# A third of w_out's K as seven block products, with sums by adding DMAs and seeded banks

## The chip, the cores and the metric

The kernel runs on one core of a Trainium2 chip. The metric is the device time of one execution in microseconds (us), as the median of three runs. One profiled execution of the same kernel gives the trace from which all rows below are read.

## The reference, cut to what matters

```
attn = windowed attention of q, k, v (4 batches, 8 heads, 576 positions, 64 wide; window 64)
x  = attn as 2304 rows of 512
g  = x @ w_gate                      # 512 -> 1536
h  = silu(g) * (x @ w_val)
x2 = h @ w_out                       # 1536 -> 512
a, b = x2 @ w1, x2 @ w2              # 512 -> 1024 each
out = ((a * b) @ w3) @ w_out2        # 1024 -> 1024 -> 512
```

The activations are float32, the weights arrive as float64. The kernel holds each value as two float32r words, a high one and a rest, and multiplies in three passes: high by high, high by rest, rest by high.

## The kernel before, in words

**Stages.** The 2304 tokens are three *token pairs* (tp 0 to 2) of two blocks of T = 384 tokens. Attention comes first, then gated layer 1 (`gated` with silu), `project` (h times w_out), gated layer 2 (a times b), the product of w3 and w_out2 (accumulators `acc`, L992), and the final product (L1067, L1135). TensorE goes through them one after another, and DVE, ACT and the DMA queues prepare operands for it: narrow the float64 words of a weight (L194, L197, L203, L207), cast to the high word (L218), subtract to get the rest (L227), and load and store.

**Gated layers.** A unit is one pair of blocks of columns of one weight for one token pair; layer 1 has 36 units, layer 2 has 24. A unit is already computed as seven block products instead of eight (Strassen-Winograd's sums), each of two 128-deep parts by three passes, six matmuls of 128x128 by 128x384. The accumulators are PSUM banks: `al` takes products 1, 6, 7, 4 in turn, `be` takes 5 and 3, `ga` takes 2. `al` after product 1 is copied out by ACT with its sign changed (tile c11, or the h tile `ha` itself for the gate), and DVE adds `ga` to it (L681). The products of neighbouring units are interleaved by the table `AT`, so that between two products of one unit others stand. `plan.wait(self.read)` makes the program reach a modelled time, nothing more; on the chip each matmul that overwrites or adds to a bank waits for the reader of that bank.

**project.** For each token pair 12 pieces of K (f) by 4 blocks of columns (m) by 2 token blocks (x) by 3 passes: 288 matmuls at L834, all eight PSUM banks accumulating over the whole K. The rows of h come back from DRAM: `Rows.queue` loads 384 KB pieces (pl, L793, on SP's queue), ACT casts them (ph<-pl, 128x768), DVE subtracts the rest in place. There are 36 such pieces. w_out is narrowed and split while layer 1 runs, stored to DRAM (`by_wo`), and loaded again as 16 resident tiles `wo` (L1288).

**Order.** The order is written by a planner, `Plan`: it keeps a model clock for each engine, and emits jobs (with costs, ranks, due times and SBUF slots) to DVE, ACT, SP and a queue called DMA (POOL's, used for DMAs that add into SBUF, L236) as TensorE's model time advances; `plan.need` forces a job that TensorE needs now. SP's DMAs go round a ring of eight: each waits for the one issued eight earlier. Each engine's instructions then stand in this order.

Of the kernel before, what the change touches and what calls it, by code (L numbers as in the profile page):

```python
# [17 lines left out]
P = 128  # L18
# [15 lines left out]
AT = {1: 0, 2: 2, 5: 3, 6: 4, 7: 8, 4: 12, 3: 13}  # L34
# [3 lines left out]
def window_attention_moe_kernel(ctx: ExitStack, tc: tile.TileContext, q, k, v, w_gate, w_val, w_out, w1, w2, w3, w_out2, out):  # L38
# [13 lines left out]
    NSLOT = 56  # L52
# [5 lines left out]
    half = ctx.enter_context(tc.tile_pool(name="half", bufs=7))  # L58
# [27 lines left out]
    class Job:  # L86
        def __init__(self, fn, after=(), cost=None, lag=0.0, rank=0, slots=0, due=0.0, early=False):

            self.rank, self.slots, self.due, self.early = rank, slots, due, early
            self.fn, self.after, self.cost, self.lag, self.done = fn, [x for x in after if x], cost, lag, None  # L90

    class Plan:
        def __init__(self):
            self.now, self.since, self.ahead, self.queue = 0.0, 0.0, 0.0, []
            self.free = dict.fromkeys(engines, 0.0)
            self.shut = set()
            self.rank, self.landing, self.early = 0, 6.0, False

            self.slots, self.keep = NSLOT - ATTENTION, 0

        def job(self, fn, after=(), lag=LAG, slots=0, due=0.0, early=False, **cost):
            j = Job(fn, after, cost, lag, self.rank, slots, due, early)
# [14 lines left out]
        def emit(self, j, e):  # L117
            start = max([self.free[e], self.since] + [x.done for x in j.after])
            self.queue.remove(j)
            j.fn(engines[e])  # L120
# [8 lines left out]
        def fill(self, but):  # L129
            limit = self.now + self.ahead  # L130
            while True:
                best = None
                for e, free in self.free.items():
# [3 lines left out]
                    for j in self.queue:  # L137
                        if e not in j.cost or (j.early and e == "DVE" and not self.early) or any(x.done is None for x in j.after):
                            continue
                        if j.slots and self.slots < j.slots + self.keep:  # L140
# [35 lines left out]
    def pool(n):  # L176
        return 0.1 + 0.0026 * n
# [7 lines left out]
    def narrow(part, load, due):  # L185
# [7 lines left out]
        n = 512  # L193
# [17 lines left out]
    def cast(hi, src, after, n, slots=1, negate=False, due=0.0):  # L211
        def fn(eng):
# [4 lines left out]
            else:  # L217
                (eng.copy if eng is nc.scalar else eng.tensor_copy)(out=hi(), in_=src())  # L218
        return plan.job(fn, after, slots=slots, due=due, early=True, ACT=act(n), DVE=0.1 + 0.0006 * n,
                        **({} if negate else {"POOL": pool(n)}))  # L220

    def rest(lo, src, hi, after, n, slots=0, negate=False, due=0.0):
        if negate:
# [4 lines left out]
                        after, slots=slots, due=due, DVE=dve(n), POOL=pool(n))  # L228

    def combine(out, x, y, op, after, n, due=0.0):  # L230
        return plan.job(lambda eng: eng.tensor_tensor(out=out(), in0=x(), in1=y(), op=op), after, due=due,  # L231
                        DVE=dve(n), POOL=pool(n))
# [5 lines left out]
    def loading(fn, after=(), slots=0, lag=9.0):  # L238
        return plan.job(fn, after, lag=lag, slots=slots, SP=0.5)
# [4 lines left out]
    class Doubles:  # L244
# [26 lines left out]
        def narrowed(self):  # L271
            return [narrow(lambda j=j: self.st[:, 512 * j:512 * j + 512], self.loaded[j], self.due) for j in range(2)]
# [4 lines left out]
    class Weights(Doubles):  # L277
# [19 lines left out]
        def make(self):  # L297
# [7 lines left out]
            for p in PRODUCTS:  # L305
                after, due = ready if p in sums else [ready[at[p][1] - 1]], self.due + AT[p]
                if p in sums:
                    x, y, op = sums[p]
                    after = [combine(lambda p=p: self.words(*at[p]), lambda x=x: self.words(*x),
                                     lambda y=y: self.words(*y), op, after + [made.get({6: 5, 3: 6}.get(p))], n, due)]  # L310
# [5 lines left out]
                         [a], n, not (p == 3 and self is left2[max(left2)]), p == 4, due)  # L316
# [9 lines left out]
    class Operands:  # L326
# [5 lines left out]
        def __init__(self, x, name, after=None, by_dma=(), rest_by_dma=(), due=0.0):  # L332
# [9 lines left out]
            for p in PRODUCTS:  # L342
                for m in range(2):
                    wait, when = [after[p]] if after else [], due + AT[p]
                    if p in sums:
# [4 lines left out]
                                combine(to, to, of, ALU.add, wait, T, when)]  # L350
# [11 lines left out]
                    else:  # L362
                        b = rest(lo, lambda m=m, p=p: blk(m, *at[p]), hi, [a], T, due=when)
# [271 lines left out]

    def gated(xop, left, order, func, hd, events, apart=0):
# [20 lines left out]
        class Unit:  # L657
# [26 lines left out]
            def put(self, i, t, src):  # L684

                h, direct = self.h(i, t), (i, t) == (1, 0)
                if self.x and direct:
# [8 lines left out]
                elif direct:  # L696
                    negated(h, src)
                    plan.charge("ACT", act(T))
# [8 lines left out]
            def product(self, p):  # L707
                if p == 1:
# [5 lines left out]
                    self.c11 = self.own(0, 0, "c11")  # L714
                    later(1, lambda: self.copy(self.c11, self.al))
                elif p == 2:
                    ga = bank(f"ga{self.name}")[:, :T]
                    self.mm(ga, 2, True)
                    self.add(self.c11, self.c11, ga)
# [732 lines left out]
```

## Time and profile before

| what | value |
|---|---|
| median of 3 runs | 825.04 us (824.42 to 825.47) |
| span of the profiled execution | 822.8 us |
| time around that span, by the median | about 2.2 us |
| TensorE (PE) busy | 811.8 us, 99% |
| VectorE (DVE) busy | 637.4 us, 77% |
| ScalarE (ACT) busy | 455.1 us, 55% |
| GpSimd (POOL) busy | 90.8 us, 11% |
| bytes moved by DMA | 140.23 MB |

The page of the profile gives the span from the first to the last instruction. The profiled execution has no time of its own beside the span; the difference to the median of the runs is taken as the launch and end, the same before and after.

### The profile page before, as it was taken

Reading aid. Unit: us, or ns where it says so; the run is one execution under the profiler, and the core shown is the slowest. Engines: PE = TensorE matmul, PEld = TensorE weight load, DVE = VectorE, ACT = ScalarE, POOL = GpSimd, SP = SyncE. Lnnn points to the kernel's source line nnn. Section 1 sums busy time; section 2 is a strip of 40 time slices with the busy share of each in tenths; the row PEclk is TensorE's granted clock in tenths of the full one; section 3 lists DMA queues with packets and bytes.
Section 4 is the critical chain, followed back from the end, with each engine's and each line's share of the span. In section 5 each row is a group of like instructions: output and inputs, shape, how many; then the busy total and the mean of one; then the engine's idle time right before and its main releaser. Section 6 shows DMA issues by size and latency. Waiting matters only on the chain.

```text
span 822.8 us, 15571 instructions
## 1 busy us (share of the span) xinstructions
PE 811.8 (99%) x5702; PEld 783.5 (95%) x5702; DVE 637.4 (77%) x1353; ACT 455.1 (55%) x1194; POOL 90.8 (11%) x135
## 2 busy tenths in 40 slices
PE   7999999999999999999999999999999999999998
PEld 5777899999999999999999999999999998899997
DVE  5899898686887959866888683877888844789994
ACT  6899997555556445633663551444444423655543
POOL 3666842000000000000000000000010110000000
PEclk9999999999999999999999999999999999999999
DMA  9999295253562444599987712024565289107632
GB/s 187 195 200 197 46 238 113 90 192 129 192 222 79 148 154 179 210 360 403 373 264 175 231 57 103 29 83 134 166 205 157 108 295 325 37 3 207 182 71 78
DMA packets 172765, 140.23 MB, mean 170 GB/s; under 512 B 120848, under 2 KB 142608, under 8 KB 171664
## 3 DMA queue, kind: packets, MB, share of 16 engines
q1 hardware_dynamic: 167888, 125.86, 50.6%
q0 software_dynamic: 4800, 13.37, 5.9%
q8 instruction: 45, 0.74, 0.4%
q14 instruction: 32, 0.26, 0.1%
HBM read 92.27 MB, written 42.99 MB: 164 GB/s over the span
## 4 chain that ended last, share of the span: by engine, by line
PE 91%; ACT 4%; SPq 2%; DMA 2%; DVE 1%; issue 0%; POOL 0%; ACTq 0%
PE o L834 18%; PE ala L669 15%; PE alb L669 15%; PE bea L669 8%; PE beb L669 8%; PE acc L992 5%; PE al L1135 4%; PE gaa L669 4%; PE gab L669 4%; ACT pexp L480 2%; PE be L1135 2%; PE al L1067 2%; PE PV L519 1%; SPq L403 1%; PE be L1067 1%; PE ga L1135 1%
## 5 line engine op out<-in xcount | busy, mean ns | idle before, releaser
L834 PE MATMUL o<-ph,wo 128*128 128x384 f32 x576 | 146.2, 334 | 0.0
L834 PEld LDWEIGHTS o<-ph,wo 128*128 128x128 f32 x576 | 103.9, 188 | 0.0
L834 PE MATMUL o<-pl,wo 128*128 128x384 f32 x288 | 96.2, 334 | 0.0
L377 ACT ACTIVATE ha<-ala 128x384 f32<-128x384 f32 x102 | 49.5, 489 | 50.1 <-PE ala L669 49.5
L759 POOL DMA_DIRECT2D h<-ha x24 | 13.0, 544 | 548.2 <-DVE ha L691 548.2
L681 DVE TENSOR_TENSOR ha<-ha,bea 128x384 f32<-128x384 f32 x60 | 33.1, 551 | 38.5 <-PE bea L669 22.1
L834 PEld LDWEIGHTS o<-pl,wo 128*128 128x128 f32 x288 | 54.1, 188 | 0.0
L480 ACT ACTIVATE pexp<-S,stat 128x128 f32<-128x128 f32 x144 | 53.3, 428 | 0.0
L218 ACT CAST hf<-h 128x384 fp32r<-128x384 f32 x84 | 38.7, 514 | 14.4 <-DVE h L231 13.6
L694 ACT ACTIVATE ha<-ha 128x384 f32<-128x384 f32 x54 | 28.3, 526 | 32.4 <-DVE ha L681 32.4
L227 DVE TENSOR_TENSOR hf<-h,hf 128x384 fp32r<-128x384 f32 x84 | 42.2, 545 | 4.9 <-ACT hf L218 4.8
L227 DVE TENSOR_TENSOR pl<-pl,ph 128x768 fp32r<-128x768 f32 x36 | 33.4, 953 | 13.2 <-ACT ph L218 12.8
L218 ACT CAST ph<-pl 128x768 fp32r<-128x768 f32 x36 | 29.2, 837 | 25.1 <-DMA pl<-h 22.6
L490 POOL TENSOR_TENSOR pexp<-pexp,stat 128x384 f32<-128x384 f32 x48 | 39.0, 833 | 36.4 <-DVE stat L487 18.0
L377 ACT ACTIVATE c12b<-alb 128x384 f32<-128x384 f32 x30 | 14.8, 493 | 50.3 <-PE alb L669 50.0
L480 ACT ACTIVATION_READ_ACCUMULATOR pexp<-S,stat 128x1 f32 x144 | 38.1, 267 | 0.0
L681 DVE TENSOR_TENSOR c22b<-c22b,beb 128x384 f32<-128x384 f32 x30 | 16.6, 553 | 25.8 <-ACT c22b L377 25.8
L669 PE MATMUL ala<-xo,w_g_7h 128*128 128x384 f32 x120 | 30.3, 336 | 0.5 <-ACT ha L377 0.5
L473 DVE TENSOR_REDUCE stat<-S 128x3 f32<-128x384 f32 x48 | 24.4, 550 | 7.6 <-PE S L466 7.4
L669 PE MATMUL ala<-xo,w_g_1h 128*128 128x384 f32 x126 | 29.2, 335 | 0.0
L218 ACT CAST xp<-X 128x384 fp32r<-128x384 f32 x42 | 19.7, 519 | 10.9 <-DVE X L231 8.0
L377 ACT ACTIVATE c11b<-alb 128x384 f32<-128x384 f32 x30 | 14.7, 489 | 19.5 <-PE alb L669 19.5
(625 smaller groups left out, 2453.2 us busy)
## 6 DMA issues: line engine op xcount, KB each, us to landing
h<-ha SPq DMA_DIRECT2D x36, 384.0 KB, 3.0
pl<-h SPq DMA_DIRECT2D x36, 384.0 KB, 6.3
h<-ha POOLq DMA_DIRECT2D x24, 384.0 KB, 3.2
h<-h SPq DMA_DIRECT2D x24, 384.0 KB, 6.4
st_w<-in_moe_w_dram SPq DMA_DIRECT2D x8, 1024.0 KB, 6.5
st_wo<-in_moe_w_out_dram SPq DMA_DIRECT2D x6, 1024.0 KB, 5.1
wo<-by_wo SPq DMA_DIRECT2D x12, 512.0 KB, 4.1
st_g<-in_moe_w_gate_dram SPq DMA_DIRECT2D x5, 1024.0 KB, 5.2
```

The source lines that it names most:

```text
L218: (eng.copy if eng is nc.scalar else eng.tensor_copy)(out=hi(), in_=src())
L227: return plan.job(lambda eng: eng.tensor_tensor(out=lo(), in0=src(), in1=hi().bitcast(F32), op=ALU.subtract), after, slots=slots, due=due, ...
L377: nc.scalar.mul(out=out, in_=in_, mul=-1.0)
L480: nc.scalar.activation(out=pe[:, jj, :], in_=so[:, jj, :], func=AF.Exp, bias=st[:, 0, x, jj:jj + 1], accum_out=st[:, 1, x, jj:jj + 1])
L490: nc.gpsimd.tensor_tensor(out=pe, in0=pe, in1=st[:, 3, x, :].unsqueeze(2).to_broadcast([P, SUB, P]), op=ALU.mult)
L669: nc.tensor.matmul(acc, lhsT=self.wt.ops[p, x][:, m, :], rhs=self.xs.ops[p, m][:, y, :], start=start and n == 0, stop=n == 5, skip_group_c ...
L681: nc.vector.tensor_tensor(out=out, in0=x, in1=y, op=ALU.add)
L694: nc.scalar.activation(out=h, in_=src, func=func, scale=-1.0 if direct else 1.0)
L834: nc.tensor.matmul(acc[m, x], lhsT=wos.tiles[i // 6][:, i % 6, :], rhs=rows[2 * tp + x].words(f, b), start=f == n == 0, stop=f == NF - 1 a ...
L992: nc.tensor.matmul(acc, lhsT=w3T[i][c // 3][:, x, (c % 3) * P:(c % 3) * P + P], rhs=zt[c, y], start=c == k == 0, stop=c == NI - 1 and k == 2)
L1067: nc.tensor.matmul(acc, lhsT=self.xs.ops[p, m][:, x, t * P:t * P + P], rhs=right.ops[p, m, y], start=start and n == 0, stop=n == 3 * R - 1 ...
L1135: nc.tensor.matmul(acc, lhsT=right.ops[p, m, y][:, P * k:P * k + P], rhs=self.xs.ops[p, m][:, x, :], start=bool(name) and n == 0, stop=n = ...
```

## The change

**w_out.** Of the six pairs of K (256 each) the first two (one pair of pairs, with fp 0 and 1) are multiplied as seven block products per token pair. Each product is two halves of its columns by two 128-deep parts of K by three passes, 12 matmuls; the third of K costs 7 x 12 = 84 matmuls per token pair where it cost 96 of 288. The other four pairs are multiplied plainly, block by block, 192 matmuls per token pair, and added into the same banks: `STEPS` is the order, numbers for products, pairs (i, j) for plain blocks. `ga` starts as ACT's copy of `al` after product 1, `de` as its copy after product 7. In all 276 matmuls per token pair instead of 288. The rows are now 15 pieces of 384 KB per token pair (7 products' sums and 8 plain ones), and w_out 20 tiles of 384 KB.

**The sums of h.** For fp 0 and 1, `spread` has ACT make one more copy of a block, and four DMAs that add in SBUF (on POOL's queue) make the sums, each followed by its store: 24 adding DMAs in all.

**Seeded banks in the gated layers.** From the seventh unit of each layer on, the copy of `al` after product 1 goes into the bank `ga`, and product 2 accumulates there; the DVE add of c11 falls away. `AT` now places product 5 ahead of product 2. Layer 2 needs an ACT copy for h in its place where x is 0.

**The rest.** Layer 2's operands get two sums and two rests from adding DMAs (24 more). Weights are narrowed 1024 words at a time. SBUF slots 58 instead of 56, `half` buffers 5 instead of 7. The cast and rest jobs lose POOL as a choice, which was closed to them before, too. TensorE has 36 matmuls fewer in all.

```
-AT = {1: 0, 2: 2, 5: 3, 6: 4, 7: 8, 4: 12, 3: 13}
+AT = {1: 0, 5: 2, 2: 3, 6: 4, 7: 8, 4: 12, 3: 13}
...
-    NSLOT = 56
+    NSLOT = 58
...
-    half = ctx.enter_context(tc.tile_pool(name="half", bufs=7))
+    half = ctx.enter_context(tc.tile_pool(name="half", bufs=5))
...
         def narrowed(self):
-            return [narrow(lambda j=j: self.st[:, 512 * j:512 * j + 512], self.loaded[j], self.due) for j in range(2)]
+            if self.second is None:
+                return [narrow(lambda: self.st, self.loaded[0], self.due, 1024)] * 2
...
+                    self.seeded = len(xs) > SEEDED
+                    self.ga = bank(f"ga{self.name}")[:, :T]
+                    self.c11 = self.ga if self.seeded else self.own(0, 0, "c11")
                     later(1, lambda: self.copy(self.c11, self.al))
+                elif p == 2 and self.seeded:
+                    plan.wait(self.read)
+                    self.mm(self.ga, 2)
+                    self.put(0, 0, self.ga)
...
+    def spread(fp, tp, h):
...
+        twice = plan.job(copy, [now], ACT=act(T))
+        first = put((1,), lambda: h00, [now])
+        both = put((2, 3), lambda: h[1].rearrange("p (c t) -> p c t", c=2), [now])
+        s5 = gather(lambda: h01, lambda: h00, [twice], 0.0)
+        s7 = gather(lambda: extra[0], lambda: h11, [twice], 0.0)
+        p5 = put((5,), lambda: h01, [s5])
+        put((7,), lambda: extra[0], [s7])
+        s6 = gather(lambda: h11, lambda: h01, [s5, s7, both], 0.0)
+        put((6,), lambda: h11, [s6])
+        s4 = gather(lambda: h10, lambda: h11, [s6], 0.0)
+        p4 = put((4,), lambda: h10, [s4])
...
+            def evict(e, m):
+                if e == 1:
+                    seed(ga, al, m, "ga")
+                elif e == 6:
+                    copy(0, 1, al, m)
+                elif e == 7 and PLAIN:
+                    seed(de, al, m, "de")
...
+    STEPS = [1, 5, 6, 7, 2] + list(BLOCKS[:2]) * bool(PLAIN) + [4] + list(BLOCKS[2:]) * bool(PLAIN) + [3]
...
-    on(events1, last1 - 2, lambda: make_to(wo[-1]))
-    on(events1, last1 - 1, lambda: project_loads(0, range(1)))
-    on(events1, last1, lambda: project_loads(0, range(1, NF2)))
+    on(events1, last1 - 2, lambda: [weight_loads(n) for n in range(3)])
+    on(events1, last1, lambda: (share(), project_loads(0)))
...
+    for n in range(3, len(STEPS)):
+        on(events_p, (0, n - 3), lambda n=n: weight_loads(n))
```

**Where instructions stand now.** First TensorE, in a late unit of layer 1 (gate, fp 5, tp 2; the letters of a name are the bank, `a` or `b` for gate or value, `xo2_20` is the operand of product 2 of tp 2). Before:

```order
L669 MATMUL ala5_2_4566<-xo2_10_2394,w_g5_1h_4326 128x384 x3
L669 MATMUL ala5_2_4566<-xo2_11_2417,w_g5_1h_4326 128x384 x3
L669 MATMUL ala5_1_4490<-xo1_70_2383,w_g5_7h_4391 128x384 x2
L669 MATMUL ala5_1_4490<-xo1_70_2383,w_g5_6l_4402 128x384
L669 MATMUL ala5_1_4490<-xo1_71_2405,w_g5_7h_4391 128x384 x2
L669 MATMUL ala5_1_4490<-xo1_71_2405,w_g5_6l_4402 128x384
L669 MATMUL gaa5_2_4585<-xo2_20_2430,w_g5_1h_4326 128x384 x2
L669 MATMUL gaa5_2_4585<-xo2_20_2430,w_g5_4h_4360 128x384
```

And now:

```order
L675 MATMUL ala5_2_4716<-xo2_10_2364,w_g5_1h_4269 128x384 x3
L675 MATMUL ala5_2_4716<-xo2_11_2372,w_g5_1h_4269 128x384 x3
L675 MATMUL alb5_1_4645<-xo1_70_2328,w_v5_7h_4552 128x384 x3
L675 MATMUL alb5_1_4645<-xo1_71_2367,w_v5_7h_4552 128x384 x3
L675 MATMUL bea5_2_4736<-xo2_50_2406,w_g5_4h_4281 128x384 x2
L675 MATMUL bea5_2_4736<-xo2_50_2406,w_g5_6h_4315 128x384
L675 MATMUL bea5_2_4736<-xo2_51_2446,w_g5_4h_4281 128x384 x2
L675 MATMUL bea5_2_4736<-xo2_51_2446,w_g5_6h_4315 128x384
L675 MATMUL gaa5_2_4723<-xo2_20_2381,w_g5_1h_4269 128x384 x2
L675 MATMUL gaa5_2_4723<-xo2_20_2381,w_g5_4h_4281 128x384
```

Product 2 (`gaa`) has moved one product back: two products now stand between it and product 1, where one did.

Second ACT, from the end of layer 1 into `project` (c12, c22: copies out of `al` in layer 1's last units; ph<-pl: casts of rows; the number after ph is the token pair, then the product or plain block and the pair of K). Before:

```order
L377 ACTIVATE c22b5_1_4820<-alb5_1_4716 128x384
L218 CAST ph0_0_0_4826<-pl0_0_0_4725 128x768
L218 CAST ph0_1_0_4840<-pl0_1_0_4727 128x768
L377 ACTIVATE c12b5_2_4851<-alb5_2_4794 128x384
L377 ACTIVATE c22b5_2_4892<-alb5_2_4794 128x384
L218 CAST ph0_0_1_4917<-pl0_0_1_4803 128x768
L218 CAST ph0_1_1_4929<-pl0_1_1_4805 128x768
```

And now (ga, de: the seeds; X2: results):

```order
L380 ACTIVATE c22b5_2_4844<-alb5_2_4774 128x384
L219 CAST ph0_1_0_4855<-pl0_1_0_4783 128x768
L219 CAST ph0_5_0_4864<-pl0_5_0_4785 128x768
L219 CAST ph0_6_0_4875<-pl0_6_0_4796 128x768
L219 CAST ph0_7_0_4877<-pl0_7_0_4798 128x768
L890 COPY ga0_0_4890<-o0_1_0_4883 128x384
L219 CAST ph0_2_0_4897<-pl0_2_0_4807 128x768
L890 COPY ga0_1_4907<-o0_1_1_4900 128x384
L219 CAST ph0_(0, 0)_1_4919<-pl0_(0, 0)_1_4809 128x768
L219 CAST ph0_(1, 0)_1_4922<-pl0_(1, 0)_1_4819 128x768
L219 CAST ph0_(0, 0)_2_4934<-pl0_(0, 0)_2_4821 128x768
L894 COPY X2_0_0_4879<-o0_1_0_4883 128x384
```

The first cast of `project` now comes behind the last copy of layer 1 (c22b5_2) instead of ahead of the last two, and the seeds stand among the casts.

Third SP's queue at the same place (h<-ha: stores of layer 1's h; pl<-h: loads of rows; wo<-wo: loads of w_out). Before:

```order
L1288 DMA wo2_4791<-wo_1_106 128x512
L1288 DMA wo2_4791<-wo_2_107 128x256
L793 DMA pl0_0_1_4803<-h_1_0_78 128x2x384
L793 DMA pl0_1_1_4805<-h_1_0_78 128x2x384
L1288 DMA wo3_4807<-wo_2_107 128x768
L1288 DMA wo4_4809<-wo_3_108 128x768
L1288 DMA wo5_4811<-wo_3_108 128x256
L1288 DMA wo5_4811<-wo_4_109 128x512
L793 DMA pl0_0_2_4824<-h_2_0_81 128x2x384
```

And now, from the stores of the last unit but one on:

```order
L818 DMA h_2_1_82<-ha5_1_1_4494 128x2x384
L865 DMA pl0_1_0_4783<-h_0_0_75 128x768
...
L865 DMA pl0_(0, 0)_2_4821<-h_2_0_81 128x768
L1495 DMA wo6_4892<-wo_96 128x768
L818 DMA h_2_2_83<-ha5_2_0_4714 128x2x384
L818 DMA h_2_2_83<-ha5_2_1_4715 128x2x384
L865 DMA pl0_(1, 0)_2_4909<-h_2_0_81 128x768
L865 DMA pl0_4_0_4931<-h_0_0_75 128x768
L1495 DMA wo9_4943<-wo_96 128x768
L1495 DMA wo10_4945<-wo_96 128x768
L1495 DMA wo11_4948<-wo_96 128x768
L1495 DMA wo12_4957<-wo_96 128x768
```

Rows and weights were loaded in turns while layer 1 still ran; now eight loads of rows stand behind the stores of the last unit but one, and wo9 and the next behind the stores of the last unit.

## Rows read from the trace of the kernel before

**Rows 1.** The page's first line and busy time of each engine.

```profile
span 822.8 us, 15571 instructions
...
PE 811.8 (99%) x5702; PEld 783.5 (95%) x5702; DVE 637.4 (77%) x1353; ACT 455.1 (55%) x1194; POOL 90.8 (11%) x135
```

**Rows 2.** Windows of four stages: length; busy PE, PEld, DVE, ACT, POOL; clock; DMA share; GB/s.

```profile
95.00:108.07 13.07, 12.59 (x119) 11.35 (x114) 11.02 (x27) 12.47 (x35) 7.97 (x10) 1.00 0.54 112
108.07:362.18 254.11, 254.11 (x1465) 253.68 (x1465) 201.66 (x425) 146.66 (x324) 13.09 (x15) 1.00 0.51 170
362.18:511.94 149.76, 149.76 (x865) 149.76 (x865) 106.52 (x187) 68.81 (x119) 0.00 (x0) 1.00 0.73 242
511.94:686.66 174.72, 174.72 (x1009) 174.72 (x1009) 132.54 (x278) 76.61 (x170) 11.88 (x22) 1.00 0.48 152
```

**Rows 3.** The chain that ended last: start us, us, what.

```profile
147.94 2.08 PE ala L669 x12
...
362.18 149.76 PE o L834 x864
```

**Rows 4.** Waits of PE over the whole span: total us, times, longest.

```profile
PE pm L563 <- POOL masks L553: 2.1, 1, 2.1
...
PE ala L669 <- ACT ha L377: 0.5, 1, 0.5
PE al L1067 <- DVE hf L227: 0.4, 1, 0.4
```

**Rows 5.** Groups of instructions: count, then busy us, mean ns, idle before them and releaser.

```profile
L377 ACT ACTIVATE ha<-ala 128x384 f32<-128x384 f32 x102 | 49.5, 489 | 50.1 <-PE ala L669 49.5
...
L203 ACT ACTIVATE st_wo<-st_wo 128x512 f32<-128x512 f32 x12 | 8.1, 673 | 3.9 <-DVE st_wo L197 3.9
...
L694 ACT ACTIVATE ha<-ha 128x384 f32<-128x384 f32 x54 | 28.3, 526 | 32.4 <-DVE ha L681 32.4
L227 DVE TENSOR_TENSOR pl<-pl,ph 128x768 fp32r<-128x768 f32 x36 | 33.4, 953 | 13.2 <-ACT ph L218 12.8
L218 ACT CAST ph<-pl 128x768 fp32r<-128x768 f32 x36 | 29.2, 837 | 25.1 <-DMA pl<-h 22.6
```

**Rows 6.** The adding DMAs at L236: issue ns min/median/max, and us to landing min/median/max.

```profile
L236 POOL DMA_DIRECT2D X<-X x10: 860/1112/1758, 98.6 to 127.0; - x10
...
DMA to landing us min/median/max: 3.2/4.7/6.2
```

**Rows 7.** Timeline of ACT in layer 1: start us, us, instruction, [idle before, releaser].

```profile
258.93 0.48 ACT L377 ACTIVATE c11b<-alb 128x384 f32<-128x384 f32 x1
...
265.50 0.49 ACT L377 ACTIVATE c11b<-alb 128x384 f32<-128x384 f32 x1 [1.70 <-PE alb L669]
```

**Rows 8.** Timeline of PE at the same place.

```profile
256.98 1.20 PE L669 MATMUL alb<-xo,w_v_1h 128*128 128x384 f32 x6
...
264.26 1.20 PE L669 MATMUL alb<-xo,w_v_1h 128*128 128x384 f32 x6
```

**Rows 9.** DMA issues over the span: count, KB each, median us to landing.

```profile
pl<-h SPq DMA_DIRECT2D x36, 384.0 KB, 6.3
...
wo<-wo SPq DMA_DIRECT2D x8, 384.0 KB, 6.0
```

**Rows 10.** Timeline of ACT where project begins.

```profile
362.84 0.83 ACT L218 CAST ph<-pl 128x768 fp32r<-128x768 f32 x1 [3.25 <-DMA pl<-h]
...
367.99 0.84 ACT L218 CAST ph<-pl 128x768 fp32r<-128x768 f32 x1 [3.30 <-DMA pl<-h]
```

**Rows 11.** Windows at the start of project, columns as in rows 2.

```profile
362.00:372.00 10.00, 10.00 (x60) 10.00 (x59) 6.30 (x10) 3.35 (x4) 0.00 (x0) 1.00 1.05 390
372.00:382.00 10.00, 10.00 (x60) 10.00 (x59) 6.42 (x12) 3.85 (x6) 0.00 (x0) 1.00 1.04 400
```

**Rows 12.** Timeline of SP where project begins: DMA issues.

```profile
356.85 1.18 SPq L793 DMA_DIRECT2D pl<-h  x2
358.13 2.57 SPq L1288 DMA_DIRECT2D wo<-wo  x4
360.79 1.51 SPq L793 DMA_DIRECT2D pl<-h  x2
362.88 7.21 SPq L1288 DMA_DIRECT2D wo<-wo  x9
```

More of the change, by code (lines that the diff above doesn't have):

```diff
@@ L697, in put @@
                     negated(h, src)
+                    plan.charge("ACT", act(T))
+                elif (i, t) == (0, 0) and self.seeded:
+                    nc.scalar.copy(out=h, in_=src)
                     plan.charge("ACT", act(T))
@@ new lines, in hi, with words @@
+                return self.hi[p, f]
+            a = loading(load, stored[f, self.tp, p], rows=1, lag=7.0, due=due)
+            b = cast(hi, lambda: self.lo[p, f].bitcast(F32), [a], 2 * T, 0, rows=2, due=due)
+            (a.behind, b.behind), Rows.before = Rows.before, (a, b)
+            self.jobs[p, f] = rest(lambda: self.lo[p, f], lambda: self.lo[p, f].bitcast(F32), lambda: self.hi[p, f], [b], 2 * T,
+                                   due=due, apart=f in APART)
+        def words(self, p, f, g, x):
+            return (self.lo if x else self.hi)[p, f][:, g, :]
@@ new lines, in used, with queue, load @@
+        def used(self, k):
+            plan.slots += sum(x == k for x in self.last.values())
+        def queue(self, k):
+            for c in self.needs(k):
+                if c in self.jobs:
+                    continue
+                n = min(768, 512 * len(W_AT) - 768 * c)
+                def load(eng, c=c, n=n):
+                    self.tiles[c] = slot([P, 6, P], F32R, f"wo{c}")
+                    eng.dma_start(out=self.tiles[c].rearrange("p n f -> p (n f)")[:, :n].bitcast(F32), in_=wod[:, 768 * c:768 * c + n])
+                self.jobs[c] = loading(load, list({id(j): j for j in (wo[f].stored[w] for w, f in self.parts[c])}.values()), 1, lag=7.0, due=k)
@@ new lines, in job, with words, project_loads @@
+        def job(self, w, f, x, m):
+            return self.jobs[(W_AT[w, f] + 256 * x + P * m) // 768]
+        def words(self, w, f, x, m):
+            c, o = divmod(W_AT[w, f] // P + 2 * x + m, 6)
+            return self.tiles[c][:, o]
+    def project_loads(tp):
+        keep, plan.rank = plan.rank, -1
+        rows[tp] = Rows(tp, "p")
+        for k, e in enumerate(STEPS):
+            for f in PAIRS_OF(e):
+                if e not in BLOCKS:
+                    rows[tp].queue(e, f, len(STEPS) * tp + k)
+                elif e in ((0, 0), (1, 1)):
+                    for i in range(2):
+                        rows[tp].queue((i, e[1]), f, len(STEPS) * tp + k)
+        plan.rank = keep
```

358 lines of the change are left out of this document (241 added, 117 removed).

## Prediction

> **What bounds the kernel now.** I read the page's first rows, then the stages, then the chain of waits, then each engine's waits. TensorE (PE) is busy 811.8 of 822.8 us [rows 1]. By stage it is fuller still: from 108.07 us on, layer 1, project and layer 2 have no idle TensorE at all, and the head of layer 1 has 13.07 - 12.59 = 0.48 us [rows 2]. The clock column is 1.00 in each stage, so nothing can be won there. The chain that ended last is one long string of matmuls; project is one piece of it, 864 matmuls in 149.76 us, so 0.1733 us each, and in the gated layers 12 matmuls take 2.08 us, the same 0.1733 [rows 3]. A block product of six is therefore 1.04 us. The only waits of TensorE for another engine behind attention are 0.5 us at the head of layer 1 and 0.4 us in the last product [rows 4]. Time therefore follows the count of matmuls, plus whatever new waits the change makes. What DVE, ACT and the DMAs gain is worth nothing by itself while they stay ahead.
>
> **The matmuls.** Project goes from 288 to 276 per token pair, 3 x 12 = 36 fewer. At 0.1733 us each this is **-6.24 us**. The gated layers keep their products, since a seeded bank takes work from DVE and not from TensorE. A floor is 825.04 - 6.24 = 818.8 us; the 0.48 us at layer 1's head can at best go too, 818.3 us.
>
> **What other engines lose and gain, costed at nothing.** Of layer 1's and layer 2's adds of c11, 48 go from DVE; ACT gets 9 copies more in layer 2 at 0.49 us [rows 5]. DVE is busy 201.66 of 254.11 us in layer 1 and 132.54 of 174.72 us in layer 2 [rows 2], with TensorE never behind it, so its relief shows in its own row alone. Nine more row pieces cost ACT 9 x 0.84 = 7.5 us and DVE 9 x 0.95 = 8.6 us [rows 5] in a stage where they are busy 68.81 and 106.52 of 149.76 us [rows 2]; TensorE's matmuls cover this, if each piece comes in time. Were that cover gone, each late piece would cost a cast and a rest, 1.8 us. The fewer `half` buffers and the narrowing of 1024 words at a time also lie behind matmuls; the second makes one ACT instruction of two of 0.67 us [rows 5], which I count below where something stands behind it.
>
> **New waits, each with its bounds.** They are estimates from rows, in the order of the program.
>
> *Layer 1's head.* Product 2 now stands after product 5, and its operand's rest comes from an adding DMA whose issue stands 28 matmuls (4.85 us) ahead of its first use, where it stood 34 (5.9 us) ahead. Such a DMA lands 3.2 to 6.2 us after issue, median 4.7 [rows 6]. From nothing to 6.2 - 4.85 = 1.4 us; I take 0.4, as the median just fits.
>
> *Seeded product 2*, in 30 units of layer 1 and 18 of layer 2. Before, the copy of `al` (c11b) started 265.50 - 264.26 = 1.24 us after the product's first matmul began, and once 258.93 - 256.98 = 1.95 us after, when ACT had other work ahead [rows 7, 8]. It takes 0.49. Now product 2 needs it, and starts 3 products, 3.12 us, after product 1 began. The margin is 3.12 - 1.73 = 1.39 us, and 0.68 in the late case. At three or four places in layer 1's end the copy stands behind two instructions of 1024 words (about 1.3 us each, twice 0.67), or one and a silu (0.53), and there it can be late by 0.1 to 0.5. Behind a waiting product 2 every product on TensorE waits too. From 0 to 1.5 us; I take 0.3.
>
> *Project's first pieces.* The first row's load stands 9.4 us ahead of project's first matmul in the model's order (16.6 before), behind the stores of the last unit but one on SP's queue, which wait for DVE. Its cast stands 12 matmuls (2.1 us) and its rest 7 (1.2 us) ahead of use. A load takes 6.3 us to land [rows 9]; cast and rest take 0.84 + 0.95 [rows 5]. 9.4 - 6.3 - 1.8 leaves 1.3 us. Before, two of project's early casts waited 3.25 and 3.30 us for loads with no loss to TensorE, as the pieces were far ahead of use [rows 10]; now the cushion is smaller. From 0 to 2.0 us; I take 0.4.
>
> *w_out's tiles 9 to 14.* They stand behind the stores of the last unit (wait for DVE) and two loads of rows on SP's queue, and are used 10.4 to 14.0 us into project. In this stretch the DMA engines are full: share 1.05 and 1.04, 390 and 400 GB/s [rows 11], so one 384 KB piece takes about 1.0 us, and SP issued nine in 7.21 us [rows 12]. Ten loads from -9.4 us on (eight rows and wo6, one at a time) keep the engines busy to about 0; after the stores and two more rows wo9 goes out at about 3 to 4 us and lands 6.0 later [rows 9], at 9 to 10, against 10.4. The next five follow at about 1.0 us and are used at 0.4 to 1.2. From 0 to 2.0 us; I take 0.7.
>
> *Copies of `al` in project.* Product 7 may write into `al` only when ACT has copied it for X2 after product 6; the copy (0.49) can stand behind one cast (0.84), 1.33 us against a distance of 1.04, so up to 0.3 us, at one or two places in each token pair. From 0 to 1.0; I take 0.4.
>
> *Rows of the plain block (1, 1).* In tp 1 the cast stands level with its use in the order, so its time depends on ACT being ahead of TensorE. It is idle more than half of that stage [rows 2]. From 0 to one cast and rest, 1.8 us; I take 0.3.
>
> **Sum.** 825.04 - 6.24 + 0.4 + 0.3 + 0.4 + 0.7 + 0.4 + 0.3 = 825.04 - 6.24 + 2.5 = **821.3 us**. The profiled execution spans 822.8 us, 2.2 below the median of runs; the same sum gives it a span of 819.1 us. 0.2% of the time (1.65 us) is about what a measurement of this kernel tells from no change.
>
> **Adding DMAs for h and layer 2** are costed at nothing in this sum. Each of six units has a chain of three (5 or 7, then 6, then 4). An issue took POOL 0.86 to 1.76 us, landing 4.7 [rows 6], so about 3 x (0.86 + 4.7) = 17 us for a chain. The products 5, 6, 7, 4 of these blocks are used in project, and the last of these units with fp 0 or 1 ends far ahead of that; so the sums hide under layer 1's matmuls. What they can hold up is SBUF slots and SP's queue, where stores wait for them with loads of weights behind; that is rival B.
>
> **Rivals.**
>
> *A: the start of project is bound by DMA.* For it: 390 to 400 GB/s at share 1.04 already [rows 11], and tp 0 now loads 35 pieces of 384 KB (15 of rows, 20 of w_out) instead of 28, about 2.75 MB more, 7 us at 395 GB/s. Against it: later tiles are needed as late as 40 us in, and before, with the engines just as full, TensorE lost nothing. If 4 us show: 821.3 + 4 = 825.3 us. It begins when wo9 lands more than about 4 us late. The Trainium skill (DMA: Bandwidth & Descriptors, section "Where 436 GB/s comes from") names about 358 GB/s as the HBM side's limit per core; this trace shows 390 and 400 GB/s and so disagrees here, and by the page's figure the pieces would come some 10% later, about 2 us at the twentieth (an estimate from that page), which leans to this rival.
>
> *B, on the other side: h's sums by adding DMAs come late.* Place: layer 1's third to twelfth units. Were landings 6.2 us [rows 6] and the POOL issues 1.76, a chain is 24 us; its tiles keep two slots for each unit that much longer, and SP's stores that wait for it hold up loads of weights behind them. A weight's load, narrowing, cast and rest that comes late stops TensorE for the whole lateness. Against it: weights are loaded well ahead of use, and SP is held for one chain at a time. It decides from about 8 us of waits in all (two weights 4 us late), where the 6.24 are gone: 821.3 + 6.5 = 827.8 us. The Trainium skill (SBUF — State Buffer, section "Who interferes with whom") says that a DMA issued through GpSimd can be starved by DVE instructions that hold the shared ports; in this trace issues took 0.86 to 1.76 us beside a DVE that is 79% busy in layer 1, so a doubling is seen, and the rule speaks for this rival.
>
> *C: no new wait shows.* All the margins above hold as in the kernel before: 818.8 us.
>
> **Chances.** The forecast (819.4 to 823.4) 0.70; C 0.10; A 0.12 (of which 0.09 within 0.2% of before, 0.03 above); B 0.08. So faster 0.80, same 0.10, slower 0.10. The range takes the forecast, C and the nearer half of A: 818.4 to 824.6 us.
>
> **What would show it.** Right: project about 143.5 us + 1 to 3 us; layer 1 254.11 us and at most 1.5 more; the list of TensorE's waits with `o` or `ga` on ACT, and `o` on DMA of `wo`, each below 1 us. Rival A: a wait at tiles `wo` or rows `ph` of 3 us or more within the first 20 us of project. Rival B: waits on weights (w_g, w_v) in layer 1 with the windows there longer by more than 3 us. Wrong: a clock column below 1.00 where TensorE has new gaps, or a matmul pitch that is not 0.173 us with the copies in PSUM.

## The result: 836.0 us instead of 825.3, slower by 1.4%

The changed kernel takes 835.98 us (median of four runs, 835.71 to 839.16), the kernel before 825.25 in the same four rounds. The ratio is 1.0137 (95% interval 1.0116 to 1.0158). The profiled execution is the slowest of the four (839.16, span 837.5); the others span 833.9 to 834.4, so some 3 us of what its trace shows come and go. The loss by the medians is 10.7 us; the trace below accounts for the 14.7 us of its own, slower execution.

Windows of the changed kernel, columns as in [rows 2]: layer 1 with its head, project, layer 2.

```profile
96.77:371.03 274.26, 268.18 (x1577) 264.57 (x1573) 200.05 (x390) 161.61 (x359) 42.64 (x48) 1.00 0.71 208
371.03:526.08 155.05, 148.44 (x829) 146.18 (x829) 105.52 (x149) 82.11 (x142) 12.75 (x15) 0.98 0.82 259
526.08:701.37 175.29, 175.29 (x1010) 174.84 (x1010) 121.76 (x229) 81.98 (x176) 20.68 (x32) 1.00 0.59 173
```

Layer 1 begins 1.6 us later than before (96.77 against 95.18, a scatter: 93.7 to 96.8 over all kernels here, whose attention is the same but for buffers). From there to project it takes 274.26 us where it took 266.84 (95.18 to 362.02), 7.4 more. Project takes 155.05, where 149.76 less 6.24 is 143.52: 11.5 lost. Layer 2 takes 0.4 to 0.6 us more, the rest the same 136.3. Together 1.6 + 7.4 - 6.24 + 11.5 + 0.4 = 14.7, the difference of the spans.

The waits of PE, columns as in [rows 4]:

```profile
PE de L932 <- ACT ph_(1, 1)_2_5194 L219: 3.7, 1, 3.7
...
PE ala L675 <- ACT ha L380: 3.3, 3, 1.4
...
PE de L932 <- DVE pl_(1, 1)_2_5600 L227: 1.1, 1, 1.1
PE gaa L675 <- ACT gaa L380: 1.1, 1, 1.1
PE ala L675 <- DVE xo L227: 1.0, 2, 0.6
...
PE ga L932 <- DMA wo<-wo: 0.8, 2, 0.6
...
PE gaa L675 <- DMA xo<-X: 0.6, 1, 0.6
```

A gap costs more than its row. The list counts from the modelled end of the last matmul, 0.33 us after its start, though in an unbroken stream the next matmul starts 0.173 us after that start; and the first matmul after the gap is slow. Two rows of PE's timeline in project with the ones around show it:

```profile
383.93 0.34 PE L932 MATMUL ga<-ph_(1, 0)_1_4922,wo 128*128 128x384 f32 x1
384.86 0.44 PE L932 MATMUL ga<-ph_(0, 0)_2_4934,wo 128*128 128x384 f32 x1 [0.59 <-DMA wo<-wo]
385.14 0.34 PE L932 MATMUL ga<-pl_(0, 0)_2_4821,wo 128*128 128x384 f32 x1
```

From 383.93 to 385.14 two matmuls took 1.21 us instead of 0.35: 0.86 lost for a gap of 0.59, so 0.27 on top. Layer 1 has seven gaps of 5.98 us in all, project seven of 6.62. Of project's, 3.69 and 0.55 are the row of block (1, 1) of tp 0, and 0.18 and 1.12 the same row of tp 1.

The largest is followed by a clock step. Windows around it:

```profile
371.03:405.03 34.00, 32.92 (x187) 31.96 (x186) 22.90 (x28) 17.25 (x26) 0.00 (x0) 1.00 1.00 384
405.00:409.00 4.00, 0.36 (x3) 0.04 (x1) 2.52 (x4) 2.44 (x4) 0.00 (x0) 1.00 1.02 407
409.00:417.00 8.00, 7.40 (x25) 7.14 (x26) 5.12 (x6) 3.30 (x4) 0.00 (x0) 0.57 0.96 361
```

TensorE stood still for nearly all of 405 to 409, and in the next 8 us its granted clock was 0.57 of full on average: most of the stretch at the lower level (1.2 of 2.4 GHz), worth 0.43 x 8 = 3.4 us.

Why the row for this matmul came late is read from SP's queue:

```profile
387.82 0.32 SPq L865 DMA_DIRECT2D pl_(0, 1)_2_5018<-h  x1
388.80 1.31 SPq L1412 DMA_DIRECT2D zd<-by_z  x2
390.70 0.38 SPq L263 DMA_DIRECT2D st_z<-in_moe_w_out_dram  x1
398.44 1.37 SPq L1412 DMA_DIRECT2D zd<-by_z  x2
399.86 0.45 SPq L263 DMA_DIRECT2D st_z<-in_moe_w_out_dram  x1
400.40 1.00 SPq L865 DMA_DIRECT2D pl_(1, 1)_2_5130<-h  x1
```

and from ACT's timeline:

```profile
408.17 0.83 ACT L219 CAST ph_(1, 1)_2_5194<-pl_(1, 1)_2_5130 128x768 fp32r<-128x768 f32 x1 [0.90 <-DMA pl_(1, 1)_2_5130<-h]
```

The load stands behind stores of w_out2's split words (zd), which wait for DVE: SP's queue issues nothing from 391.08 to 398.44 (the row of its waits for these stores over the whole span is below). The load goes out at 400.40 and lands at 408.1, 7.7 us later, for a matmul that PE reaches at 405.2. All this time the DMA engines are full (share 1.00, 384 GB/s).

```profile
SPq L1412 <- DVE by_z L227: 22.1, 6, 10.8
```

### The profile page after: what moved, and what is told of

Read it like the earlier page. It is cut to its first block, busy times and chain, and to the rows that moved or that the text cites. A ratio compares the mean times of both kernels' runs of the same rounds, so it can differ in the third digit from the quotient of the medians.

```text
span 837.5 us, 15624 instructions
## 1 busy us (share of the span) xinstructions
PE 813.7 (97%) x5666; PEld 780.6 (93%) x5666; DVE 612.5 (73%) x1204; ACT 476.3 (57%) x1224; POOL 134.0 (16%) x183
## 4 chain that ended last, share of the span: by engine, by line
PE 81%; DMA 7%; SPq 4%; DVE 3%; ACT 2%; issue 2%; POOL 1%; DVEq 0%; ACTq 0%; POOLq 0%
PE ala L675 13%; PE alb L675 13%; PE o L932 8%; PE bea L675 7%; PE beb L675 6%; PE acc L1087 5%; PE al L1230 4%; PE gab L675 3%; PE gaa L675 3%; PE de L932 3%; SPq L406 2%; PE ga L932 2%; PE be L1230 2%; PE al L1162 2%; PE PV L522 2%
## 5 line engine op out<-in xcount | busy, mean ns | idle before, releaser
L236 POOL DMA_DIRECT2D X<-X x22 | 24.8, 1217 | 278.4 <-DVE xp L227 272.1
L380 ACT ACTIVATE ha<-ala 128x384 f32<-128x384 f32 x78 | 38.0, 488 | 28.3 <-PE ala L675 27.7
L932 PE MATMUL o<-ph,wo 128*128 128x384 f32 x144 | 37.7, 334 | 0.0
L380 ACT ACTIVATE c12b<-alb 128x384 f32<-128x384 f32 x30 | 14.7, 491 | 25.7 <-PE alb L675 25.7
L694 DVE SCALAR_TENSOR_TENSOR ha<-alb,ha 128x384 f32<-128x384 f32 x30 | 16.7, 555 | 16.3 <-PE alb L675 16.2
L675 PE MATMUL alb<-xo,w_v_1h 128*128 128x384 f32 x120 | 26.6, 334 | 0.0
L932 PEld LDWEIGHTS o<-ph,wo 128*128 128x128 f32 x144 | 26.1, 188 | 0.0
L236 POOL DMA_DIRECT2D ha<-ha x18 | 16.3, 924 | 61.0 <-ACT hs L836 23.4
L508 DVE COPY ptt<-PT 128x384 f32<-128x384 f32 x48 | 23.8, 537 | 2.2 <-PE PT L502 2.2
L932 PE MATMUL o<-pl,wo 128*128 128x384 f32 x72 | 24.2, 336 | 0.3 <-DVE pl L227 0.3
L219 ACT CAST xo<-X 128x384 fp32r<-128x384 f32 x41 | 20.6, 533 | 6.4 <-DMA xo<-X 5.4
```

The lines of the kernel that those rows point to most:

```text
L236: return plan.job(lambda eng: eng.dma_start(out=out(), in_=x(), accum_op=ALU.add), after, lag=4.5, due=due, DMA=1.0)
L380: nc.scalar.mul(out=out, in_=in_, mul=-1.0)
L675: nc.tensor.matmul(acc, lhsT=self.wt.ops[p, x][:, m, :], rhs=self.xs.ops[p, m][:, y, :], start=start and n == 0, stop=n == 5, skip_group_c ...
L932: nc.tensor.matmul(to[m], lhsT=wos.words(w, 2 * f + g, x, m), rhs=rows[tp].words(row, f, g, y), start=start and f == g == n == 0, stop=g = ...
```

## The experiments

Times are medians; "layer 1" is the length from its first matmul to project's, "project" that to layer 2's (274.3 and 155.1 in the changed kernel, 266.8 and 149.8 before). Beside each run stands the kernel before, run on the same chip (medians 824.1 to 825.2). A length of a stage is that of one profiled execution, and it scatters: the changed kernel and three whose program differs from it only from about the end of layer 1 on show 274.3, 274.2, 275.5 and 276.9 us for layer 1. Every edit also moves other instructions in the planned order.

**Seeds alone, in the kernel before.**

```
-AT = {1: 0, 2: 2, 5: 3, 6: 4, 7: 8, 4: 12, 3: 13}
+AT = {1: 0, 5: 2, 2: 3, 6: 4, 7: 8, 4: 12, 3: 13}
...
+                    self.seeded = len(xs) > SEEDED
```

> The kernel before with the seeded banks and the moved product 2 alone (48 DVE adds fewer, w_out as before). Theory W (the loss lies in w_out's block products and what they move, the seeds are harmless): 825 to 826.5, TensorE's gaps in layer 1 below 2 us. Rival (seeds cost layer 1 its 6 us): 829 to 832.

825.48 us, ratio 1.0012 (1.0001 to 1.0022); layer 1 268.4. By themselves the seeds cost about 1.5 us of layer 1, and DVE's relief (637.4 to 615.4 us busy) brings nothing. The theory's range held: the rest of the loss shows only where w_out's products are.

**Twice as many block products.**

```
-    SEVEN = 2
+    SEVEN = 4
```

> The changed kernel with two thirds of K in block products instead of one: 36 matmuls (6.24 us) fewer again, 48 adding DMAs for h instead of 24, 18 pieces of rows per token pair instead of 15, 24 tiles of w_out instead of 20. Theory D (the loss comes with each block product's sums, rows and tiles): slower still, 842 to 855, with waits on rows and tiles in project. Rival (a loss paid once): 829 to 832.

845.85 us. Project is shorter than in any other kernel, 143.8 us, and layer 1 longer, 292.3. A window of its layer 1:

```profile
93.95:386.23 292.28, 273.31 (x1576) 267.26 (x1572) 205.25 (x408) 166.11 (x372) 63.44 (x72) 0.99 0.82 232
```

The time is inside the theory's range, but its place is mostly layer 1, not project, and there the loss grows with the products. DMA share is 0.82 there, 0.71 in the changed kernel and 0.51 before [rows 2].

**h's sums on DVE.**

```
-        s5 = gather(lambda: h01, lambda: h00, [twice], 0.0)
+        s5 = combine(lambda: h01, lambda: h01, lambda: h00, ALU.add, [twice], T)
```

(and the other three in the same way)

> The changed kernel with h's four sums made by DVE adds (24 of 128x384, 0.55 us each, 13 us of DVE in layer 1) instead of 24 adding DMAs on POOL's queue. The changed kernel's profile has layer 1's gaps at 5.98 us. Theory L (POOL's queue runs in order, so layer 1's own adding DMAs for xo and the tiles that h's chains hold come late): the gaps between 110 and 215 us (0.56, 0.47, 0.60, 1.39, 0.88) go but for 0.5 at the head, and the time falls by 3 to 4 us, to about 832. Rival (the gaps come from ACT, which has the seeds and 1024-word instructions to do): they stay, and DVE's 13 us more add to them, 836 to 838. Project's gaps stay in both.

840.92 us, above both ranges. The gaps at 134 and 140 us (0.60 and 1.39) are gone, a new one of 0.50 stands at 142, and the one ahead of them grew from 0.47 to 0.97. But a sum made in place writes over a block that a store still reads: the add waited for that store (6.87 us of DMA h<-ha on the chain that ended last), and behind it came a gap of 4.61 us at 210 us with a stretch at half clock. So this doesn't tell what the adding DMAs cost.

**h's sums left out.** The four sums are not made; all copies, stores and loads stay. Then the same without seeds.

```
-        s5 = gather(lambda: h01, lambda: h00, [twice], 0.0)
-        s7 = gather(lambda: extra[0], lambda: h11, [twice], 0.0)
+        s5 = s7 = twice
...
-        s6 = gather(lambda: h11, lambda: h01, [s5, s7, both], 0.0)
+        s6 = twice
...
-        s4 = gather(lambda: h10, lambda: h11, [s6], 0.0)
+        s4 = twice
```

> The changed kernel with the 24 adding DMAs for h left out (the four sums are not made; the blocks are stored unsummed in their places, all stores and loads stay). Theory L2 (layer 1's 7 us of new stalls come from chains of adding DMAs: POOL's queue holds up xo's, SP's queue stands 53 us for h's stores, slots are held): layer 1 falls from 274.3 to 268 to 270 us, the time to 830 to 832. Rival (they come from the ordering and the work on w_out's words): layer 1 stays above 272 us and the time above 834.

> The changed kernel without seeded banks (48 DVE adds back, product 2 where it was). Theory S (the wait of product 2 for ACT's copy costs something): the 1.09 us gap at 334 us goes and little else, 834.5 to 835.5. Rival (seeding relieves DVE so much that without it layer 1 is later): 837 to 840. Rival (seeding causes most of layer 1's 6 us): about 830.

> The changed kernel without seeded banks and with the 24 adding DMAs for h left out (the four sums are not made). With one of the two edits layer 1 was 272.5 and 273.0 us long, from 274.3. If two causes hide behind one another: 268 to 270 us of layer 1, as with the stores on POOL's queue and no seeds. If the adding DMAs hardly count: 271.5 to 272.5 us.

Sums left out: 833.16 us, layer 1 273.0. Seeds left out: 834.95 us, layer 1 272.5. Both: 830.90 us, layer 1 267.7, 0.8 us from the kernel before. Windows of layer 1, in this order:

```profile
94.51:367.55 273.04, 268.08 (x1576) 264.51 (x1573) 199.03 (x390) 159.93 (x358) 21.04 (x24) 1.00 0.60 192
```

```profile
95.43:367.90 272.47, 267.88 (x1577) 264.60 (x1573) 212.52 (x419) 160.73 (x356) 41.97 (x48) 1.00 0.71 207
```

```profile
95.22:362.90 267.68, 266.65 (x1576) 264.68 (x1573) 212.46 (x419) 160.90 (x358) 21.03 (x24) 1.00 0.61 195
```

Either edit gives back 1 to 2 of the 7.4 us in layer 1, both together 6.6. Sums left out missed the theory (268 to 270 us) and met half of the rival; seeds left out met the theory's time (834.5 to 835.5), and the gap at 334 us is gone, but one of 1.15 stands at 336. Both edits together are what gives layer 1 back. That the two causes hide behind one another (3.0 us one by one, 6.6 together) is suggested and not shown: single traces of layer 1 scatter by 2.8 us, and by the medians, each against the kernel before beside it, the loss of 10.7 us falls by 2.6, 0.9 and 4.6.

How the sums and the adding DMAs get to TensorE is shown for two gaps, by ACT's timeline ahead of them in the changed kernel, and TensorE's:

```profile
138.71 0.51 ACT L219 CAST xo<-X 128x384 fp32r<-128x384 f32 x1 [5.38 <-DMA xo<-X]
139.55 0.47 ACT L380 ACTIVATE ha<-ala 128x384 f32<-128x384 f32 x1
140.07 1.31 PE L675 MATMUL ala<-xo,w_g_7h 128*128 128x384 f32 x6 [1.39 <-ACT ha L380]
```

```profile
213.18 0.42 ACT L219 CAST w_v_7h<-st_v 128x256 fp32r<-128x256 f32 x1 [2.61 <-DMA ha<-ha]
213.50 0.48 ACT L380 ACTIVATE ha<-ala 128x384 f32<-128x384 f32 x1
214.03 1.32 PE L675 MATMUL ala<-xo,w_g_7h 128*128 128x384 f32 x6 [0.88 <-ACT ha L380]
```

At 138.71 a cast has waited 5.38 us for an adding DMA of xo, and the copy out of `al` that TensorE needs stands behind it on ACT; at 213.18 the cast of a weight has waited 2.61 us for a sum of h, and the copy that ends TensorE's 0.88 us gap stands behind it. In the trace of the kernel before, no instruction waited for an adding DMA. POOL's own queue stood still for h's sums from 96 to 220 us (total, times, longest):

```profile
POOL ha L236 <- DMA ha<-ha: 20.9, 6, 6.0
```

But xo's DMAs do not come late by that queue alone: with the sums left out and the seeds in, TensorE's wait for xo (0.60 us at 134) is 1.60:

```profile
PE gaa L675 <- DMA xo<-X: 1.6, 1, 1.6
```

SP's waits from 100 to 370 us, in the changed kernel and with sums and seeds left out:

```profile
SPq L818 <- DMA ha<-ha: 48.1, 15, 8.2
SPq L818 <- DVE ha L697: 44.9, 6, 16.7
```

```profile
SPq L818 <- DVE ha L697: 63.0, 11, 18.8
```

With sums and seeds left out the row for sums is gone, but the row for h itself has grown, and all rows together come to 227 us in both kernels (250 before). So this list doesn't show SP's queue as the path.

**h's stores on POOL's queue.** The stores of the four sums go out behind the adding DMA that each waits for.

```
-        p5 = put((5,), lambda: h01, [s5])
+        p5 = put((5,), lambda: h01, [s5], DMA=1.0)
```

> The changed kernel with the stores of h's four sums issued from POOL's queue behind the adding DMA that each waits for, so that SP's queue no longer stands still for them (53 us of such waits in layer 1). Theory Q (loads of weights behind them on SP's queue are late): layer 1's gaps at 214 and 334 us (0.88, 1.09) go, 833 to 835. Rival (layer 1's gaps come from POOL's queue itself): they stay or grow, as POOL's queue has 24 stores more and its chains get longer, 836 to 840.

834.08 us, which is in the theory's range for another reason: project was shorter (151.5). Layer 1 takes 274.9, no gain there. The 0.88 at 214 is a 1.03 in another place, the 1.09 at 333 stays, and the wait for xo grew from 0.60 to 1.37.

**Narrowing by 512 words.**

```
-            if self.second is None:
-                return [narrow(lambda: self.st, self.loaded[0], self.due, 1024)] * 2
```

> The changed kernel with weights narrowed by 512 words at a time again (twice as many instructions of 0.68 instead of 1.2 us). Theory (the long instructions delay copies that TensorE waits for): the gaps of ACT's copies, 1.09 at 334 us and part of 0.88 at 214 us, go; 834 to 835. Rival (no effect): 836. Rival (more instructions on DVE): 837.

839.29 us, above all three forecasts. The 1.09 at 334 us is gone, a 2.17 at 215 us has come; layer 1 275.0.

**w_out2's work later**, by seven steps of project and by three.

```
-    on(events_p, (0, 1), lambda: (setattr(plan, "landing", 8.0), make_to(w3s[NW3 - 1])))
+    on(events_p, (0, 1), lambda: setattr(plan, "landing", 8.0))
+    on(events_p, (0, 8), lambda: make_to(w3s[NW3 - 1]))
```

> The changed kernel with the narrowing, splitting and storing of w_out2 and w3 begun seven steps of project later (about 31 us). Theory P (in project SP's queue stands behind stores of that work, and the DMA engines are full, so rows of block (1, 1) come 4 us late): the 3.69 + 0.55 us gap at 405 to 410 us falls below 1 us, and with it the seven us at half clock behind it, so 836 becomes 829 to 831. Rival (the rows are late by the bandwidth of w_out's 20 tiles alone): the gap stays above 3 us, 835 to 836. Second rival (the work is only moved to where it delays layer 2's operands or the final product): project is 5 us shorter and the time behind it longer by as much.

> The changed kernel with the work on w_out2 and w3 begun three steps later instead of seven (about 14 us). Theory P (a crowd at the start of project and enough room behind it): the 3.69 us gap is gone and tp 2's rows and layer 2's weights are in time, 829 to 833. Rival (project as a whole has too little room for it on SP's queue and the DMA engines): gaps of 1 to 3 us stay at either place, 836 to 840.

Seven steps: 840.13 us. Project's first 34 us:

```profile
369.34:403.34 34.00, 33.50 (x190) 32.52 (x190) 16.46 (x20) 14.48 (x23) 0.00 (x0) 1.00 0.85 332
```

The DMA share there is 0.85, not 1.00, and the gap at block (1, 1) of tp 0 is gone. But rows of tp 2 are late (1.54 and 1.58 us at 503 to 505), then a weight of layer 2 (2.65 at 529), with a stretch at half clock behind the rows and one behind the weight; project takes 152.6 us, layer 2 179.7, so the second rival comes nearest. The edit takes work off SP's queue and off the DMA engines at once, so it doesn't tell the two apart. With three steps the DMA engines are full again (share 1.01, 388 GB/s), the gap is 1.73 + 0.55 us, the clock stays at 1.00 behind it, and project takes 149.7: 834.12 us, between the two ranges.

**Rows on POOL's queue**, which is empty in project.

```
-            a = loading(load, stored[f, self.tp, p], rows=1, lag=7.0, due=due)
+            a = plan.job(load, stored[f, self.tp, p], lag=7.0, rows=1, due=due, DMA=0.5)
```

> The changed kernel with the 45 loads of h's rows issued from POOL's queue, which is empty in project, instead of SP's. Theory H (a row of block (1, 1) is late because stores of w_out2's words stand ahead of it on SP's queue and wait): its load goes out some 6 us earlier, the 3.69 us gap is gone, project falls from 155 to 149 us or less, 830 to 832. Rival (the DMA engines are full at 385 GB/s and all comes late by that): the load goes out earlier and lands as late, or tiles of w_out are later for it; the gap or one of its size stays, 834 to 837.

843.00 us, as the rival has it, but worse. No row is late any more, but tiles of w_out are: 6.40, 1.67 and 1.18 us, all in project's first 26 us. Its first 34 us:

```profile
372.44:406.44 34.00, 24.65 (x109) 22.52 (x109) 17.21 (x22) 12.32 (x19) 6.63 (x13) 0.75 1.01 391
```

The bytes per second (391) are those of the other kernels with full engines (384 and 388) and the lateness is on other pieces. So taking the row out from behind the waiting stores is not enough: the order of the queues decided what was late, and with full engines and these pieces something was.

**Together.** Stores and rows on POOL's queue and w_out2's work three steps later (with seeds, and without); then the stores on POOL's queue, no seeds, and w_out2's work three steps later, five steps, three steps with half of w3 moved on into layer 2, and five steps with seeds in layer 2 alone.

> Three of these together: h's sums stored from POOL's queue, rows loaded from POOL's queue, w_out2's work three steps later. If each takes away a wait of its own: 828 to 831. If it is one limit (the DMA engines) that shows in turn at other places: 832 to 835. Below 825 is not expected, as layer 1's new stalls stay.

> The same without seeded banks. If what the seeds cost beside w_out's products (0.5 to 1.5 us, measured alone) comes off: 827 to 830. If DVE's 48 adds are missed: above the kernel with seeds.

> The changed kernel with three edits: no seeded banks, h's sums stored from POOL's queue, w_out2's work three steps later; rows stay on SP's queue. If layer 1's stalls (274.3 us long, 269.0 with the first two edits together) and project's (155.1, 149.7 with the third) are separate and add: 95 + 269 + 149.7 + 175.4 + 136.3 = 825.4 us of span, 826 to 828. Rival (they trade with one another): 831 or more.

> The same with w_out2's work five steps later. If project's first 34 us are bound by the DMA engines and each thing taken out of them counts: no gap at block (1, 1) of tp 0, project 146 to 148 us, 823 to 826. Rival (what is put off comes back as late rows of tp 2 and late weights of layer 2, as with seven steps): 828 to 832.

> As the first of these, with two of the four pieces of w3 that are made in project moved into layer 2. If project as a whole is short of DMA time: 1 to 2 us less than the first. Rival (the crowd is at the start alone, which this doesn't touch): the same within 1 us.

> As the version with three edits and w_out2's work five steps later (829.7 us), with seeded banks in layer 2 again and none in layer 1. If the seeds help layer 2 (175.1 us long with them in the changed kernel, 177.4 without in that version): 2 us less, 827 to 828.5. Rival (layer 2 was late by w3's delayed work and its adding DMAs): the same within 1 us. Neither gets below the kernel before.

| version | us | layer 1 | project | layer 2 |
|---|---|---|---|---|
| rows too, seeds | 842.60 | 273.6 | 158.3 | 175.1 |
| rows too, no seeds | 834.62 | 269.0 | 153.8 | 175.4 |
| no seeds, three steps | 832.01 | 271.2 | 152.9 | 176.7 |
| no seeds, five steps | 829.74 | 269.7 | 150.6 | 177.4 |
| no seeds, three steps, w3 on | 830.96 | 269.6 | 149.9 | 179.0 |
| seeds in layer 2 only, five steps | 829.76 | 271.1 | 151.8 | 175.7 |

The first two lie outside their ranges, 842.60 far above. The three-step version was to show that the two losses add (826 to 828); it took 832.01, the rival's time, though its runs go from 827.4 to 835.7 (822.3 to 825.4 for the kernel before beside it), so this is not decided. Five steps (829.74) is in its rival's range too, w3 moved on is 1.05 us below the three-step version, which that scatter covers, and seeds in layer 2 alone change nothing, as their rival said. The five-step version has a ratio of 1.0073 (1.0057 to 1.0088) to the kernel before, about half the loss: each of the two losses was cut. But project never came below 149.7 with a third of K in products, 6 us above its matmuls, and what was put off showed in layer 2. No version beats the kernel before.

## Why the prediction was wrong

**The matmuls.** -6.24 us was right: project has 36 matmuls fewer, and its length is 143.5 us and its stalls.

**The step that failed: project's rows of block (1, 1).** The four terms for project's rows, tiles and copies were priced at 0.4 + 0.7 + 0.4 + 0.3 = 1.8 us and measured 11.5. The tiles of w_out (0.7) and the first row (0.4) came near: 0.59 + 0.19 and 0.30 in the list. The copies of `al` (0.4) show no row at all. Rows of block (1, 1) were priced at 0.3, with one cast and rest as the upper bound, for tp 1 only and by ACT's idle share. They cost 3.69 + 0.55 in tp 0 and 0.18 + 1.12 in tp 1; with 0.27 for each gap and 3.4 for the clock that is about 10 of the 11.5 us. The wait of tp 1, which was foreseen, was mis-sized; the larger one, of tp 0, has no term, since a load's place in the model's order was taken for the time at which it goes out. It stood behind stores that wait on SP's queue (7.4 us without an issue) and took 7.7 us to land. The bound should have come from the landing under full engines, and from what stands ahead on SP's queue.

**Rival A was nearer, and mispriced.** It said that full DMA engines make the start of project late, from 825.3 us, chance 0.12. The run with rows on another queue (lateness moved to tiles at the same GB/s) speaks for it, and the one with w_out2's work later (share 0.85, gap gone) fits it. Its sign, a wait of 3 us or more within project's first 20 us, was not met: the wait came 34 us in. Before, the same 34 us ran at 401 GB/s with no TensorE idle (columns as in [rows 2]):

```profile
362.02:396.02 34.00, 34.00 (x198) 34.00 (x198) 21.46 (x34) 13.73 (x19) 0.00 (x0) 1.00 1.04 401
```

There the pieces are needed evenly over the token pair, and now all but product 3's within its first 33 us or so. That I saw the bytes and not when they are due is why the chance was low. Its price of 4 us lacked the clock: gaps of 3.69 + 0.55 cost 3.4 us more.

The Trainium skill (DMA: Bandwidth & Descriptors, section "Where 436 GB/s comes from") puts the HBM limit per core at about 358 GB/s, a stack's 716 GB/s over two cores. The traces hold 384 to 401 GB/s over 34 us with one core at work, and the measurement decides: the 10% that the prediction worked out from that figure has no part in this.

**Layer 1's terms** (0.4 for the head, 0.3 for seeded product 2) measured 7.4 together with the adding DMAs, costed at nothing. The named waits are there, and larger: 0.56, 0.47 and 0.60 for xo at the head, 1.63 where 1.4 was the bound, and 1.09 for ACT's copy behind 1024 words at 334 us. The other 3.26 us of gaps (0.99, where it was 0.48 before, 1.39 and 0.88) are waits for ACT's copy of `al` for h, which no term has. Layer 1 without seeds and sums is 267.7 us long, so 6.6 us belong to the two. Without w_out's products the seeds cost 1.5. "TensorE never behind it" held for the kernel before; that both edits use up the same margin fits the lengths, and is argued.

**Rival B** had the place, h's sums in layer 1, with a chance of 0.08, and in part the way: the cast of a weight waits for a sum (2.61 us). But its sign was not met, as no wait of TensorE on w_g or w_v is in the list; the delay came through ACT's copies. With twice the products such a wait is there (2.23 us at 349 us, for w_v_1h). That its 6.5 us is close to layer 1's 7.4 - 0.7 = 6.7 is luck, since the seeds have their part in that. A and B came together; the rivals were priced one at a time, though both rest on DMAs that the same edit adds. (Their parts make "same" 0.09 and "slower" 0.11, where the prediction has 0.10 each.)

The Trainium skill (SBUF — State Buffer, section "Who interferes with whom") says that DVE can starve a DMA issued through GpSimd. The prediction saw that in issues of 0.86 to 1.76 us, but most of the longer ones go with something else. In the changed kernel an issue took 0.86 us where POOL's last one had ended, and longer nearly always where it had not:

```profile
123.60 0.86 POOL L236 DMA_DIRECT2D xo<-X  x1 [4.16 <-ACT xo L362]
124.29 1.06 POOL L236 DMA_DIRECT2D ha<-ha  x1
125.06 1.17 POOL L236 DMA_DIRECT2D hs<-ha  x1
125.60 1.52 POOL L236 DMA_DIRECT2D X<-X  x1
126.30 1.72 POOL L236 DMA_DIRECT2D xo<-X  x1
126.83 2.07 POOL L236 DMA_DIRECT2D X<-X  x1
```

Only one of 56 (1.46 us, at 147.57) is much longer with nothing ahead of it. The landings took 3.0, 4.6 and 8.4 us (min, median, max); what made the longest was not tried.

**Left open.** Which of POOL's queue, SP's queue and slots held by a chain does most in layer 1: two gaps are traced to waits of ACT for adding DMAs, moving the stores alone gained nothing, and how the seeds and the sums act together was not followed. Whether the waiting stores or the full DMA engines made the row of tp 0 late was not tried apart. Why layer 2 takes 175.4 us in one version without seeds and 176.1 to 179.0 in the others was not followed.

## What to carry to other kernels

When TensorE is 99% busy, a change that trades matmuls for sums, stores and loads spends the slack of every queue it touches; price it by when each new piece is due against bytes at the measured rate, not by the mean share of the stage. A place in the planned order is not an issue time where a queue waits in order: read what stands ahead of it and what that waits for. Two edits that each fit in the margin may not fit together; undo both before you acquit either, and take more than one trace where a stage's length scatters by more than the effect.

## What the runs showed of the hardware

A gap of TensorE costs about 0.27 us beyond its row, by the one worked out above. In or behind every gap of 2.65 us or longer in these traces, from layer 1 on, (2.65, 2.78, 2.79, 2.99, 3.39, 3.62, 3.69 and longer) the granted clock was 0.50 for the next few us. Behind those between 1.4 and 2.4 us it fell in some cases (1.41 at 459 us with narrowing by 512 words, 1.93 at 214 with rows on POOL's queue, 2.41 at 312 with twice the products) and not in others (2.13 at 255 with twice the products, 2.41 at 660 with w3 moved on). With rows on POOL's queue, where tiles came late one after another, it stayed low from 386 to 403 us. From layer 1 on, all stretches below 1.00 fell where TensorE waited, but for the last few us of a program.

An adding DMA's issue takes POOL 0.86 us alone and up to 2.07 us when six follow closely. With the DMA engines full (share 1.00), loads of 384 KB issued from 380 to 388 us in the changed kernel took 7.7 to 9.1 us to land, where the median before was 6.0 to 6.3 [rows 9].
